# Attention and feed-forward on one core: two weight chunks begun later, and a group's last quarter product done in halves

## The chip, the cores and the metric

The kernel runs on one core of a Trainium2 chip. The metric is the device time of one execution in microseconds (us). The time of a kernel is the median of several executions; besides them there is one execution under the hardware profiler, which gives the profile and the trace.

The core has five engines that run their own instruction queues in order: PE (TensorE, matmuls), DVE (VectorE), ACT (ScalarE), POOL (GpSimd) and SP (SyncE, here only an issuer of DMAs). They meet at semaphores: an instruction that needs another engine's result waits at the head of its queue, and all behind it waits too. Matmul results land in PSUM[...].

## The reference

```python
scores = scale * np.matmul(q, k.transpose(0, 1, 3, 2))          # (8, 8, 576, 576)
thresh = np.max(scores, axis=-1, keepdims=True) - tau
scores = np.where(scores >= thresh, scores, -1000000000.0)
scores = scores - np.max(scores, axis=-1, keepdims=True)
attn = np.exp(scores)
attn = attn / (np.sum(attn, axis=-1, keepdims=True) + 1e-09)
x = np.matmul(attn, v)                # then heads side by side: (8, 576, 512)
xn = (x - mu) / np.sqrt(var + 1e-06) * g_ln
out = x + np.maximum(xn @ w_ch1, 0.0) @ w_ch2                   # 512 -> 2048 -> 512
```

There are 8 batches of 8 heads with 576 tokens of 64 features, in float32. The mean and the variance go over the 512 features of a token. The two weight matrices come in as 64-bit values and have to be turned into float32 on the chip, once.

## The kernel before, in words

**Slots.** A batch has nine slots, so there are 72 slots, n = 0 to 71. Each slot has the scores of a part of the queries for two heads (`scores`, L404; the scores of all slots lie in the same PSUM banks), their maxima and exponentials (`exponentials`, L427, four ACT instructions e0 to e3), thresholds and sums (`weights`, L451: four DVE instructions "STT", L456, which read the scores a second time), and in the next slot the turned weights times v. In the first slots of the kernel the weights are turned on PE: the products named tr and tp go to PSUM and ACT copies them to the tiles em (L500, L506) that the values' product reads. In later slots this goes through a DRAM scratch, scr.

**Groups.** The feed-forward part works on 16 groups g of 288 tokens (two per batch). `first_part` (L781) makes 16 tiles of hidden, each four products p1 and a ReLU on ACT (L801). Group 0 then multiplies with w2 in the plain way (`second_plain`). All other groups use `second_quarters` (L844): w2 and hidden are each seen as 2 x 2 quarters, and seven products of quarters (a scheme of Strassen's kind) take the place of eight. They are the seven calls of `segment`: w2[0,0], w2[0,1], s3, s2, w2[1,1], w2[1,0], and s4 last, where s2, s3, s4 are differences of w2's quarters. Each `segment` is a sum over d = 0..7 for two tiles m = 0, 1 of 144 columns, both in one PSUM bank; a `product` is two instructions of 64 rows and [...] a segment has 64 matmul records in the trace. ACT copies the whole bank out (L896). In the last group, g = 15, the s4 segment is instead multiplied by the root of the variance on DVE (`times_root`). The pool `ps_ff`, from which the segments, p1, the means and the variances take their PSUM banks, holds two.

Additions of the seven results to the quarters of y (u2, u3, u4, 11, 12, 21, 22), the scaling and the residual (`finish`) and the transposes for the output (`store`, into tiles ot, L722) are put off: `later` hangs them on a list, `drops`, with an engine and a cost, and `drip` takes a few from it at fixed places of a slot (with everything=True all of them). `send` (L725) issues four DMAs for each 128 features. They go on SP's queue; for the last group they are spread over SP, ACT and POOL.

**Order.** The order is written out by hand in the main loop (L1062 to L1148): each engine's queue has the instructions in the order in which that code emits them. Each slot has four positions, and at each `second_part` (L993) lets the feed-forward steps of the current group run, as many as a budget says. Where a slot's parts are put off into the next slot, `at_quarter` notes the position, and `run` emits them there. In slots 1 to 4 some products on constants (`constants`, L1054) stand ahead of the scores.

**Weights.** Class `Weights` (L178) converts 32 chunks of 512 columns, 16 of w1 and then 16 of w2. One chunk is a load on SP (`fetch`), two DVE instructions (`begin`, L274 and L278), two ACT instructions (queued by `begin`, L284 and L287, let go by `flush`), an addition on POOL (`carry`, L299), a mask on DVE (`mask`, L308) and, for w1 only, a scaling on POOL (`scale`, L320). Table `BEGUN` (L1049) says for each slot how many chunks are begun by three positions of the slot: ahead of the STTs, behind them (there the next slot's scores run on PE), and at the slot's end. Masks are emitted ahead of the STTs (L1093) and behind them (L1108). A group's products wait for the chunks they need.

Of the kernel before, what the change touches and what calls it, by code (L numbers as in the profile page):

```python
# [12 lines left out]
ALU = mybir.AluOpType  # L13
# [5 lines left out]
def kernel(  # L19
# [76 lines left out]
    def product(out, lhsT, rhs, **flags):  # L96


        for h in range(2):
            r = slice(64 * h, 64 * h + 64)  # L100
            nc.tensor.matmul(out[r], lhsT=lhsT[:, r], rhs=rhs, **flags)  # L101
# [325 lines left out]
    def exponentials(n):  # L427


        neg = small.tile([128, 4], F32, tag="neg", name="neg")  # L430
        thr = small.tile([128, 4], F32, tag="thr", name="thr")
        es = e_room[(n + 1) % 2 if n < SLOTS else 0]
        for h in range(2):
            i = slice(2 * h, 2 * h + 2)
            nc.vector.tensor_reduce(  # L435
                out=neg[:, i], in_=pairs[h],
                axis=AXL.X, op=ALU.max, negate=True,
            )
            nc.gpsimd.tensor_scalar(  # L439
                out=thr[:, i], in0=neg[:, i], scalar1=-1.0, scalar2=low_sb,  # L440
                op0=ALU.mult, op1=ALU.add,
            )
            if h == 0:
                run(n, "copy")
                conversion.scale_all()
        for i in range(4):
            if i == 2:
                yield es, thr
            nc.scalar.activation(es[:, i], blocks[i], func=AF.Exp, bias=neg[:, i : i + 1])  # L449

# [237 lines left out]
    def drip(room=None, everything=False):  # L688


        urgent = [i for i, d in enumerate(drops) if d[0]]
        n = urgent[-1] + 1 if urgent else 0
        room = dict(room or {})
        while drops:
            _, when, eng, cost, go = drops[0]
            if n <= 0 and not everything:
                if when == now or room.get(eng, 0) < cost:
                    break
                room[eng] -= cost
            drops.pop(0)  # L700
            n -= 1
            go()
# [17 lines left out]
    def store(eng, g, m, o):  # L720
        ot = ffn.tile([128, TOK], F32, tag="o", bufs=4, name="ot")
        eng.transpose(ot, o)  # L722
        stores.append(lambda: send(g, m, ot))

    def send(g, m, ot):  # L725
        b, t = divmod(g, 2)
        for i in range(4):
            f = m * 128 + 32 * i
            eng = nc.sync
            if g == NG - 1:  # L730
                eng = (nc.sync, nc.gpsimd)[m % 2] if m >= HM else (nc.sync, nc.scalar)[i % 2]
            eng.dma_start(
                out=out[b, t * TOK : (t + 1) * TOK, f : f + 32].rearrange(
                    "(n r) c -> r n c", r=32
                ),
                in_=ot[32 * i : 32 * i + 32].rearrange("p (n c) -> p n c", c=32),
            )
# [106 lines left out]
    def second_quarters(g, rb):  # L844

        s2, s3, s4 = more
        b11, b12 = hidden[:, :HD, early], hidden[:, :HD, late]  # L850
        b21, b22 = hidden[:, HD:, early], hidden[:, HD:, late]
        drip(everything=True)
        y = ffn.tile([128, NK, TOK], F32, tag="sq", bufs=1, name="y")
        part_of = lambda t, i, j: t[:, HM * i : HM * i + HM, (early, late)[j]]
        y11, y12, y21, y22 = (part_of(y, i, j) for i in range(2) for j in range(2))
        done = set()

        def later(*calls, urgent=None):
            for what, cost, fn, eng, *args in calls:

                def go(what=what, fn=fn, eng=eng, args=args):
                    fn(eng, *args)
                    done.add(what)

                drops.append((urgent, now, eng, cost, go))

        def need(*what):
            while not done.issuperset(what):
                drops.pop(0)[-1]()

        def by_fours(eng, out, in0, in1, op):
            for d in range(0, HD, 4):
                at = (slice(None), slice(d, d + 4))
                eng.tensor_tensor(out=out[at], in0=in0[at], in1=in1[at], op=op)  # L874

        def times_root(out, bank):
            r = rb[:, late].unsqueeze(1).to_broadcast([128, HM, HT])
            dve.tensor_tensor(out=out, in0=bank, in1=r, op=ALU.mult)

        def segment(weights, rhs, out=None, as_it_is=False):  # L880
            bank = ps_ff.tile([128, HM, HT], F32, tag="ff", name="seg")
            for d in range(HD):
                for m in range(HM):
                    at, end = (d, m), (HD - 1, HM - 1)
                    product(
                        bank[:, m], lhsT=weights[:, m, d], rhs=rhs[:, d],
                        start=at == (0, 0), stop=at == end,
                    )
                    if at != end:
                        yield 2, 0.5  # L890
            if out is None:
                out = ffn.tile([128, HM, HT], F32, tag="part", bufs=4, name="part")
            if as_it_is:
                times_root(out, bank)
            else:
                nc.scalar.copy(out, bank)  # L896
            return out

        def add(eng, out, a, b):
            eng.tensor_tensor(out=out, in0=a, in1=b, op=ALU.add)  # L900

        def finish(eng, i, j=None):

            cols = slice(None) if j is None else (early, late)[j]
            at = (slice(None), slice(HM * i, HM * i + HM), cols)
            z, x = y[at], groups[g][at]
            r = rb[:, cols].unsqueeze(1).to_broadcast(list(z.shape))
            eng.tensor_tensor(out=z, in0=z, in1=r, op=ALU.mult)
            add(eng, z, z, x)

        dve, pool = nc.vector, nc.gpsimd
        done_by = pool if g < NG - 1 else dve
        later(("t3", 3, by_fours, pool, b12, b22, b12, ALU.subtract), urgent=pool)
        banks_taken[0] = True
        yield from segment(w2[0, 0], b11, y11)
        need("t3")
        later(("t2", 3, by_fours, dve, b11, b11, b12, ALU.add), urgent=dve)
        yield 2, 0.5
        p2 = yield from segment(w2[0, 1], b21)
        need("t2")  # L920
        later(("t4", 3, by_fours, pool, b21, b21, b11, ALU.subtract), urgent=pool)
        yield 2, 0.5
        p7 = yield from segment(s3, b12)
        yield 2, 0.5
        yield from segment(s2, b11, y21)
        need("t4")
        later(("t1", 3, by_fours, dve, b11, b22, b11, ALU.subtract), urgent=dve)
        later(
            ("u2", 1, add, pool, y21, y21, y11), ("11", 1, add, pool, y11, y11, p2),
            ("done11", 2, finish, pool, 0, 0),  # L930
        )
        yield 2, 0.5
        p4 = yield from segment(w2[1, 1], b21)
        yield 2, 0.5
        need("t1", "u2", "11")
        p5 = yield from segment(w2[1, 0], b11)
        later(
            ("u4", 1, add, dve, y12, y21, p5), ("u3", 1, add, dve, y21, y21, p7),
            ("22", 1, add, dve, y22, y21, p5), ("21", 1, add, dve, y21, y21, p4),
            ("hi", 3, finish, done_by, 1),  # L940
        )
        ends_here = g == NG - 1
        if ends_here:
            later(("done12", 2, finish, dve, 0, 1))
            later(*((f"o{m}", 1, store, dve, g, m, y[:, m]) for m in (2, 3)))
        yield 2, 0.5
        last = segment(s4, b22, as_it_is=ends_here)
        for _ in range(12):
            yield next(last)
        banks_taken[0] = False  # L950
        while waiting_mean:
            mean_of(waiting_mean.pop(0))
        p3 = yield from last
        later(("12", 1, add, dve, y12, y12, p3))
        if not ends_here:
            later(("done12", 2, finish, done_by, 0, 1))
        later(
            *((f"o{m}", 1, store, dve, g, m, y[:, m]) for m in ((2, 3, 0, 1) if g < NG - 1 else (0, 1)))
        )
        yield 2, 0.5  # L960

    def ffn_steps(g):
# [73 lines left out]
    else:  # L1036
# [10 lines left out]
        conversion.scaled = conversion.n1  # L1047

    BEGUN = [  # L1049
        (0, 0, 2), (3, 3, 4), (5, 5, 6), (7, 7, 8), (9, 9, 10), (11, 11, 12),  # L1050
        (14, 16, 18), (20, 22, 24), (26, 28, 30), (32, 32, 32),
    ]

    def constants(times):  # L1054
# [7 lines left out]
    for n in range(NS):  # L1062
# [27 lines left out]
            conversion.fetch(2)  # L1090
        if n < SLOTS + HP:
            run_all(aside)
        conversion.mask_all()  # L1093
        conversion.begin_to(masks_at)
        if n <= HP + 1:
            conversion.carry_all()
# [92 lines left out]
```

## Time and profile before

| | us |
|---|---|
| median of three executions | 1358.27 (1357.86, 1358.27, 1360.97) |
| the profiled execution | 1357.61 |
| its span, first to last instruction | 1355.8 |
| PE busy in the span | 1326.8 (98%) |
| DVE, POOL, ACT busy | 874.0, 615.3, 470.0 |
| first matmul to the end of slot-wise conversion, about | 0 to 189.3 |
| last matmul ends | 1346.33 |

The profiled execution is 1.8 us longer than its span, which runs from the first to the last instruction. The clock that the throttle granted to TensorE was 0.998 of full speed over the span.

How to read the lines of the profile. A row of the waits names an engine, what it wanted to do, and what released it; then the waited time in all, the number of waits and the longest one. A row of the timeline has a start and a length in us, engine, line, operation, output<-inputs with their sizes, the number of instructions of that kind that were put together, and in brackets the idle time just before with its releaser. L101 is the helper `product`, through which all the feed-forward products go, so these are told apart by the tile's name: p is p1 or p2, seg is a segment, mean and var are the layernorm's sums. seg<-hidden,e is the s4 segment, because s4 is kept in the room of a former e tile.

### The profile page before, as it was taken

How to read it: one execution, taken by the hardware profiler on the slowest of the kernel's cores; microseconds unless marked ns; L12 is line 12 of the kernel's file. 1: busy time of each engine (PE TensorE's matmuls, PEld its weight loads, DVE VectorE, ACT ScalarE, POOL GpSimd, SP SyncE). 2: the span in 40 equal slices, each digit the busy share in tenths (PEclk: the TensorE clock that was granted, in tenths of full speed). 3: DMA queues.
4: the chain of work that ended last, by engine and by line, in shares of the span. 5: the costliest groups of instructions: out<-in, count | busy, mean ns of one | idle time of the engine just before them, and what ended most of it. 6: DMA issues, size and time to landing. Idle time of an engine off the chain costs nothing.

```text
span 1355.8 us, 40852 instructions
## 1 busy us (share of the span) xinstructions
PE 1326.8 (98%) x17616; PEld 1003.3 (74%) x17616; DVE 874.0 (64%) x1531; ACT 470.0 (35%) x1022; POOL 615.3 (45%) x824
## 2 busy tenths in 40 slices
PE   8999999999999999999999999999999999999997
PEld 6766657869687786968778696877869687786967
DVE  7978777666755676666766667556766667665202
ACT  4877432332423323232333323233232323333120
POOL 3554455445444344444534454443444445344312
PEclk9999999999999999999999999999999999999999
DMA  9813464457644775447744576446754376443211
GB/s 172 264 52 98 122 182 148 177 159 183 190 141 142 194 197 167 150 136 183 195 149 151 150 191 180 147 146 188 201 169 150 131 189 178 144 155 131 64 19 19
DMA packets 320996, 206.88 MB, mean 153 GB/s; under 512 B 246896, under 2 KB 278384, under 8 KB 312752
## 3 DMA queue, kind: packets, MB, share of 16 engines
q1 hardware_dynamic: 314704, 203.38, 52.0%
q8 instruction: 138, 2.26, 0.7%
q10 hardware_dynamic: 5952, 0.74, 0.4%
q0 software_dynamic: 160, 0.15, 0.1%
q14 instruction: 42, 0.34, 0.1%
HBM read 120.46 MB, written 83.76 MB: 151 GB/s over the span
## 4 chain that ended last, share of the span: by engine, by line
PE 90%; DVE 3%; ACT 2%; DMA 1%; POOL 1%; issue 1%; SPq 1%; POOLq 0%; DVEq 0%; ACTq 0%
PE p L101 37%; PE seg L101 30%; PE sc L421 10%; PE sc L604 8%; PE sc L614 2%; PE tp L101 1%; ACT e L449 1%; DVE e L456 1%; PE var L101 1%; PE mean L101 1%; SPq L118 0%; DMA x_room<-in_moe_w_ch_dram 0%; ACT em L506 0%; DMA qk_room<-in_q_dram 0%; DVE w L308 0%
## 5 line engine op out<-in xcount | busy, mean ns | idle before, releaser
L101 PE MATMUL p<-xc,w 128*64 128x288 f32 x4096 | 517.4, 408 | 6.8 <-ACT part L896 4.6
L101 PEld LDWEIGHTS p<-xc,w 128*64 128x64 f32 x4096 | 287.4, 137 | 214.4 <-issue 13.5
L435 DVE TENSOR_REDUCE neg<-sc 128x2 f32<-128x1152 f32 x144 | 188.6, 1351 | 280.8 <-PE sc L421 280.2
L472 POOL TENSOR_SCALAR e<-e,den 128x576 f32<-128x576 f32 x252 | 193.6, 780 | 133.5 <-DVE den L461 133.5
L101 PE MATMUL seg<-hidden,w 128*64 128x144 f32 x3840 | 247.9, 287 | 0.0
L101 PEld LDWEIGHTS seg<-hidden,w 128*64 128x64 f32 x3840 | 234.9, 137 | 11.5 <-issue 8.5
L456 DVE SCALAR_TENSOR_TENSOR e<-sc,thr,e 128x576 f32<-128x576 f32 x288 | 221.8, 809 | 16.9 <-POOL thr L439 11.2
L801 ACT ACTIVATE hidden<-p 128x288 f32<-128x288 f32 x256 | 106.6, 417 | 303.6 <-PE p L101 303.6
L439 POOL TENSOR_SCALAR thr<-neg,low_sb 128x2 f32<-128x2 f32 x144 | 41.4, 288 | 374.4 <-DVE neg L435 374.0
L449 ACT ACTIVATE e<-sc,neg 128x576 f32<-128x576 f32 x288 | 197.9, 755 | 2.4 <-DVE neg L435 2.4
L546 DVE STREAM_TRANSPOSE et<-e 128x1152 f32<-128x1152 f32 x112 | 153.4, 1374 | 14.7 <-POOL e L472 14.2
L421 PE MATMUL sc<-kT,qT 64*64 64x384 f32 (+3 forms) x2048 | 139.4, 403 | 3.2 <-DVE e L456 2.2
L604 PE MATMUL sc<-em,v_in 128*64 128x128 f32 (+1 forms) x2368 | 129.4, 263 | 0.0
L604 PEld LDWEIGHTS sc<-em,v_in 128*64 128x64 f32 x2368 | 122.8, 137 | 7.9
L101 PE MATMUL seg<-hidden,stage 128*64 128x144 f32 x1920 | 123.3, 286 | 0.0
L101 PEld LDWEIGHTS seg<-hidden,stage 128*64 128x64 f32 x1920 | 117.6, 137 | 2.9 <-issue 2.9
L627 ACT COPY x<-sc 128x128 f32<-128x128 f32 x120 | 31.7, 266 | 238.8 <-PE sc L421 170.4
L421 PEld LDWEIGHTS sc<-kT,qT 64*64 64x64 f32 x2048 | 76.1, 133 | 44.1 <-issue 21.2
L874 POOL TENSOR_TENSOR hidden<-hidden 128x576 f32<-128x576 f32 x60 | 84.8, 1426 | 52.1 <-ACT hidden L801 42.4
L896 ACT COPY part<-seg 128x288 f32<-128x288 f32 x74 | 29.9, 404 | 190.4 <-PE seg L101 190.0
L874 DVE TENSOR_TENSOR hidden<-hidden 128x576 f32<-128x576 f32 x60 | 51.3, 889 | 51.5 <-PE seg L101 48.5
L101 PE MATMUL seg<-hidden,e 128*64 128x144 f32 x960 | 65.3, 286 | 0.0
(145 smaller groups left out, 1098.9 us busy)
## 6 DMA issues: line engine op xcount, KB each, us to landing
scr<-et SPq DMA_DIRECT2D x63, 1152.0 KB, 4.9
em<-scr SPq DMA_DIRECT2D x63, 1024.0 KB, 5.7
q_in<-in_q_dram SPq DMA_DIRECT2D x124, 72.0 KB, 2.7
out_dram<-ot SPq DMA_DIRECT2D x248, 36.0 KB, 3.8
k_in<-in_k_dram SPq DMA_DIRECT2D x120, 72.0 KB, 3.0
er<-scr SPq DMA_DIRECT2D x126, 64.0 KB, 5.2
v_in<-in_v_dram SPq DMA_DIRECT2D x28, 256.0 KB, 5.5
w<-in_moe_w_ch_dram SPq DMA_DIRECT2D x12, 512.0 KB, 4.8
```

What stands on the lines that cost most here:

```text
L101: nc.tensor.matmul(out[r], lhsT=lhsT[:, r], rhs=rhs, **flags)
L421: nc.tensor.matmul(sc[h][64 * i : 64 * i + 64, at : at + n], lhsT=ql[r] if s == HP else qT[r, half, j * 128 + 64 * i : j * 128 + 64 * i + 64],
L435: nc.vector.tensor_reduce(out=neg[:, i], in_=pairs[h], axis=AXL.X, op=ALU.max, negate=True,)
L439: nc.gpsimd.tensor_scalar(out=thr[:, i], in0=neg[:, i], scalar1=-1.0, scalar2=low_sb, op0=ALU.mult, op1=ALU.add,)
L449: nc.scalar.activation(es[:, i], blocks[i], func=AF.Exp, bias=neg[:, i : i + 1])
L456: nc.vector.scalar_tensor_tensor(out=es[:, i], in0=blocks[i], scalar=thr[:, i : i + 1], in1=es[:, i], op0=ALU.is_ge, op1=ALU.mult, accum_o ...
L472: nc.gpsimd.tensor_scalar(out=es[:, i], in0=es[:, i], scalar1=den[:, i : i + 1], scalar2=1.0, op0=ALU.mult, op1=ALU.mult,)
L546: nc.vector.transpose(et[:, :, 64 * h : 64 * h + 64].rearrange("p n (j c) -> p j n c", j=2), es[:, 2 * h : 2 * h + 2].rearrange("p j (n c) ...
L604: nc.tensor.matmul(dst[64 * h : 64 * h + 64], lhsT=vt[:, h, c, :], rhs=pick(em[:, 2 * j : 2 * j + 2, c], h), start=c == 0 and first, stop= ...
L627: nc.scalar.copy(x_of(2 * b + (s > HP))[:, s % (HP + 1), 128 * j : 128 * j + 128], pv[j])
L801: nc.scalar.activation(hidden[:, d], p1, func=AF.Relu)
L874: eng.tensor_tensor(out=out[at], in0=in0[at], in1=in1[at], op=op)
```

## The change

There are three parts.

1. `exponentials` gives control back after its third exponential, not its second, in slots 1 to 5. ACT then has e2 ahead of the copies that are emitted at the slot's first position.
2. `BEGUN` begins one chunk fewer in each of slots 1 and 2, stays two behind through slot 6, and makes up for them with a third chunk in the middle of slots 7 and 8. In slots 0 to 2 no masks are emitted ahead of the STTs; what is due there comes behind the STTs, into the gap in which the next scores run.
3. In `second_quarters` the s4 segment runs over m outside and d inside. After m = 0 is complete, `end_of_half` copies its 144 columns on ACT (line 902 of the changed kernel), and after m = 1 the other 144. In the last group each half is multiplied, added, transposed and handed to `send` at once on DVE (line 905), after all that is put off has been let go. The sums are in another order: 21 and u3 come after the p4 segment, 22 and u4 after p5, and the last group's finishes are split into three. The s2 segment is copied to y12 instead of y21. The last group's sends go to SP alone for m = 2, 3, and to SP, ACT, POOL, SP for m = 0, 1.

```diff
-            if i == 2:
+            if i == (3 if 0 < n < HP + 2 else 2):
                 yield es, thr
...
-            if g == NG - 1:
-                eng = (nc.sync, nc.gpsimd)[m % 2] if m >= HM else (nc.sync, nc.scalar)[i % 2]
+            if g == NG - 1 and m < HM:
+                eng = (nc.sync, nc.scalar, nc.gpsimd, nc.sync)[i]
...
-        def times_root(out, bank):
-            r = rb[:, late].unsqueeze(1).to_broadcast([128, HM, HT])
-            dve.tensor_tensor(out=out, in0=bank, in1=r, op=ALU.mult)
-
-        def segment(weights, rhs, out=None, as_it_is=False):
+        def segment(weights, rhs, out=None, halves=None):
             bank = ps_ff.tile([128, HM, HT], F32, tag="ff", name="seg")
-            for d in range(HD):
-                for m in range(HM):
-                    at, end = (d, m), (HD - 1, HM - 1)
-                    product(
-                        bank[:, m], lhsT=weights[:, m, d], rhs=rhs[:, d],
-                        start=at == (0, 0), stop=at == end,
-                    )
-                    if at != end:
-                        yield 2, 0.5
+            at = [(d, m) for d in range(HD) for m in range(HM)]
+            if halves:
+                at.sort(key=lambda t: t[1])
             if out is None:
                 out = ffn.tile([128, HM, HT], F32, tag="part", bufs=4, name="part")
-            if as_it_is:
-                times_root(out, bank)
+            for i, (d, m) in enumerate(at):
+                product(
+                    bank[:, m], lhsT=weights[:, m, d], rhs=rhs[:, d],
+                    start=d == 0 if halves else i == 0,
+                    stop=d == HD - 1 if halves else i == len(at) - 1,
+                )
+                if i == len(at) - 1:
+                    break
+                if halves and d == HD - 1:
+                    halves(m, out[:, m], bank[:, m])
+                yield 2, 0.5
+            if halves:
+                halves(m, out[:, m], bank[:, m])
             else:
                 nc.scalar.copy(out, bank)
             return out
+
+        def end_of_half(m, out, bank):
+            if not ends_here:
+                nc.scalar.copy(out, bank)
+                return
+            drip(everything=True)
+            dve.tensor_tensor(out=out, in0=bank, in1=rb[:, late], op=ALU.mult)
+            add(dve, y12[:, m], y12[:, m], out)
+            store(dve, g, m, y[:, m])
+            run_all(stores)
...
-        yield from segment(s2, b11, y21)
+        yield from segment(s2, b11, y12)
...
         p4 = yield from segment(w2[1, 1], b21)
+        later(("u3", 1, add, dve, y22, y12, p7), ("21", 1, add, dve, y21, y22, p4))
+        if ends_here:
+            later(("done21", 2, finish, dve, 1, 0))
...
         p5 = yield from segment(w2[1, 0], b11)
-        later(
-            ("u4", 1, add, dve, y12, y21, p5), ("u3", 1, add, dve, y21, y21, p7),
-            ("22", 1, add, dve, y22, y21, p5), ("21", 1, add, dve, y21, y21, p4),
-            ("hi", 3, finish, done_by, 1),
-        )
+        later(("22", 1, add, dve, y22, y22, p5), ("u4", 1, add, dve, y12, y12, p5))
         if ends_here:
-            later(("done12", 2, finish, dve, 0, 1))
-            later(*((f"o{m}", 1, store, dve, g, m, y[:, m]) for m in (2, 3)))
+            later(
+                ("done22", 2, finish, dve, 1, 1), ("done12", 2, finish, dve, 0, 1),
+                *((f"o{m}", 1, store, dve, g, m, y[:, m]) for m in (2, 3)),
+            )
+        else:
+            later(("hi", 3, finish, pool, 1))
         yield 2, 0.5
-        last = segment(s4, b22, as_it_is=ends_here)
+        last = segment(s4, b22, halves=end_of_half)
...
     BEGUN = [
-        (0, 0, 2), (3, 3, 4), (5, 5, 6), (7, 7, 8), (9, 9, 10), (11, 11, 12),
-        (14, 16, 18), (20, 22, 24), (26, 28, 30), (32, 32, 32),
+        (0, 0, 2), (2, 2, 3), (3, 3, 4), (5, 5, 6), (7, 7, 8), (9, 9, 10),
+        (12, 14, 16), (19, 21, 23), (26, 28, 30), (32, 32, 32),
     ]
...
-        conversion.mask_all()
+        if n >= HP - 1:
+            conversion.mask_all()
         conversion.begin_to(masks_at)
```

## Prediction

> **What bounds the kernel now.** I read the busy shares first, then the chain that ended last, then TensorE's waits, then the timeline around each place that the change touches.
>
> ```profile
> PE 1326.8 (98%) x17616; PEld 1003.3 (74%) x17616; DVE 874.0 (64%) x1531; ACT 470.0 (35%) x1022; POOL 615.3 (45%) x824
> ```
> ```profile
> PE 90%; DVE 3%; ACT 2%; DMA 1%; POOL 1%; issue 1%; SPq 1%; POOLq 0%; DVEq 0%; ACTq 0%
> ```
>
> PE is busy for 98% of the span and makes 90% of the chain. So only three things can move the time: the 1355.8 - 1326.8 = 29 us in which PE is idle, new PE idle time, and PE work (the instructions are the same in number and shape, so none). The stretches by window say where the 29 us lie: about 14.7 us before 189.3 us, 5.1 us from there to the last matmul (1157.03 - 1152.06 = 5.0 in the row of 189.30 to 1346.33), 9.5 us after it.
>
> ```profile
> PE p L101 <- ACT part L896: 4.6, 8, 0.6
> PE tr L520 <- ACT em L506: 2.8, 5, 0.7
> PE tp L101 <- ACT em L506: 2.4, 4, 0.8
> PE sc L421 <- DVE e L456: 2.2, 5, 0.6
> PE p L101 <- DVE w L308: 1.4, 1, 1.4
> ```
>
> These are TensorE's waits. In the long steady part there is one kind only, the first, eight times: a group's first product waits until ACT has copied the s4 segment out of PSUM, because the p1 and segment banks come from a pool of two. The other four kinds lie in the first 189 us. One of the eight, closer:
>
> ```profile
> 416.14 3.11 PE L101 MATMUL seg<-hidden,e 128*64 128x144 f32 x48
> 419.57 1.15 PE L101 MATMUL seg<-hidden,e 128*64 128x144 f32 x16
> 420.84 0.40 ACT L896 COPY part<-seg 128x288 f32<-128x288 f32 x1 [2.79 <-PE seg L101]
> ```
>
> The columns are start, length, engine, line and operation. This is the s4 segment: 64 matmuls of 144 columns, one each 3.11/48 = 0.065 us, with a mean product between the 48th and 49th. The next waiting product starts at 421.29. The last pair of matmuls started at 420.43, so without a wait the next would have started at 420.43 + 2 x 0.065 = 420.56: **the price of one full PE -> ACT -> PE round trip with a 128x288 copy is 421.29 - 420.56 = 0.73 us**, of which the copy itself is 0.40.
>
> **What the Trainium skill says.** "PSUM — Partial Sum Buffer", section "PSUM bank collisions raise a hardware error": two engines may not touch one bank and quadrant at once, and PSUM is to be guarded by bank and quadrant, not by address. The trace of before shows no engine reading a bank that PE still fills; the segment copy starts 0.12 us after the last matmul's end. Same page, "Engine vs sequencer instructions": matmuls start and complete in program order; so nothing queued behind a waiting one passes it, and in the trace p waits with all that follows. "Perfetto Trace Analysis", "Optimizing Scalar/DVE Operations": each ACT or DVE instruction has a fixed overhead, and larger ones are better where the engine is full, smaller ones where another waits. The trace agrees: ACT's copies from PSUM took 0.215, 0.266, 0.404 and 0.594 us at 64, 128, 288 and 512 columns. "DMA: Bandwidth & Descriptors", "Issuing engines are not separate DMA queues": issuing from several engines saves only issue time. No run shown here separates the two.
>
> **Part 1: the halves of s4 (groups 1 to 15).** Before, d ran outside and m inside, so both halves of the bank were open to the end. Now m = 0 is finished after 32 of the 64 matmuls, is copied, and m = 1 goes on in the same bank. I built the changed kernel and resolved its waits: in all 15 groups the 33rd matmul waits for that half's reader, ACT in groups 1 to 14 and DVE in the last. Before, the segment had a wait at its start only. The first 48 matmuls stand without anything between them in each of the 15 groups (the x48 row above), so nothing lies at the boundary to cover it. Cost: a round trip with a 128x144 copy. By the rows just named that copy takes about 0.28 us (between 0.266 at 128 and 0.404 at 288), so 0.73 - (0.404 - 0.28) = **0.61 us**. ACT must also be free. Half time of 416.14 is 418.2; the p5 copy of ACT started at 417.61 and took 0.44, so it is free at 418.05. In group 1 ACT is in two exponentials until 260.36 while the half ends at about 259.8 plus latency: 0.93 us. So 13 x 0.61 + 0.93 = +8.8 us. Both ends: if a wait cost only the 0.12 between matmul end and copy start, 14 x 0.12 = +1.7; if ACT is caught in an exponential (0.755 mean) in half the groups, 0.35 more for 7 of them, +11.3. I take +8.8, because the same round trip was measured eight times at 0.57 of wait, each time alike. It is partly given back: the second half's copy at the segment's end is short too, so the eight waits shown lose 0.12 each: -1.0. What moves because of the reordered sums (u3 and 21 after p4, 22 and u4 after p5) is queued on DVE at 64% with half a segment of room, and nothing on PE waits for it before the group's end: 0.
>
> **Part 2: slots 1 to 9, in order.** I followed PE's position against before. The exponential moved ahead of ACT's em copies costs 0.635 us of ACT (its pitch) wherever a transpose waits on that copy, and makes the third weight STT earlier, for which the scores wait. The masks of slots 1 and 2 go from ahead of the STTs to behind them, where DVE has nothing else until the next scores are done. A PE-bound slot of the loop (scores to turns 4.33, turns to scores 4.57, scores 2.19: 11.09, against 11.06 measured) hardly gains. Running sum: slot 2's scores -0.65 (the masks leave the way), slot 3's 0, slot 4's +0.6 (transposes wait for em behind the exponential), slot 5's 0, slot 6's -0.6, which shrinks to -0.2 where a mean waits for POOL's sum. Slot 7 gets a third conversion, one more pair of ACT instructions of 0.576 us each = 1.15, and PE was waiting on ACT here already:
>
> ```profile
> 116.47 0.46 PE L101 MATMUL p<-xc,w 128*64 128x288 f32 x2 [0.73 <-ACT hidden L801]
> ...
> 160.36 0.33 PE L520 MATMUL tr<-diag,e 128*64 128x128 f32 x2 [0.69 <-ACT em L506]
> ...
> 179.22 0.46 PE L101 MATMUL p<-hidden,w 128*64 128x288 f32 x2 [1.37 <-DVE w L308]
> ```
>
> These three are the rows of the timeline where PE waits on the conversion or beside it. After the first: +0.9. A wait of 0.77 at 153.34 goes with the earlier reduction: +0.2. In slot 9 all three last conversions (3 x 1.15 = 3.46 of ACT, where one of 1.15 stood) come between o's copy and em4's; PE there had 0.70 of slack: the second row comes at about 162, +1.7. Then the third row's 1.37 goes, since the last mask is earlier and the last load no longer stands behind an scr store on SP: **+0.3 net**. This is my least certain sum: down to -4.3 if all of DVE's waits (2.2 + 0.77 + 1.37) go and the exponential costs nothing; up to +3 if slots 7 to 9 pay for each pair.
>
> **Part 3: the end.**
>
> ```profile
> 1342.24 4.09 PE L101 MATMUL seg<-hidden,e 128*64 128x144 f32 x64
> ...
> 1347.76 5.46 SPq L732 DMA_DIRECT2D out_dram<-ot  x8
> 1348.01 0.42 DVE L878 TENSOR_TENSOR part<-seg,rb 128x288 f32<-128x288 f32 x1
> ...
> 1349.01 0.84 DVE L722 STREAM_TRANSPOSE ot<-y 128x288 f32<-128x288 f32 x2
> ```
>
> Before: PE ends at 1346.33, DVE at 1349.85, the last send is issued at about 1352.8, the span ends 3.0 later. After: DVE's queue holds, from 1342.96, the two adds, two finishes and two transposes for m = 2, 3 and only then half 0's multiply. By the durations of before that is 2 adds at 1.93/4 = 0.97, two finishes of a multiply (0.45) and an add (0.46) = 1.82, the transposes 0.83 and the half multiply some 0.3: 3.9, so it ends at about 1346.9. PE's 33rd matmul waits for it: the second half runs 1347.0 to 1349.05 (PE ends 2.7 later). Half 1's multiply, add and transpose at half size take about 1.1, so the last tile is ready at 1350.15, 0.3 later than before. But SP issues 12 sends from 1346.33 at about 0.47 each, the last near 1351.6 against 1352.8, and ACT and POOL two each: **-1.1** (from -2 to +0.5, where the late tile sets the end instead).
>
> **The sum.** 8.8 - 1.0 + 0.3 - 1.1 = +7.0 on the profiled execution's 1357.61 (span 1355.8, 1.8 around it): 1364.6. The median of the runs, 1358.27, is 0.66 above that execution; a change of 7.0 on it gives **1365.3 us**, slower by 0.5%. A measurement here tells about 0.3%, 4.1 us, from no change.
>
> **Rivals.**
> (a) Not slower: the start was bound by DVE, so the 4.3 us go and the earlier exponential is free. For: the five sc<-DVE waits are in consecutive slots, which a single queue would make. Against: tr and tp wait on ACT as often. 8.8 - 1.0 - 1.1 - 4.3 = +2.4: 1360.7. That is not slower as measured. It decides from a start gain of 2.9 us on. Chance 0.14.
> (b) The start loses 3 more, as the ACT pairs of slots 7 to 9 stand ahead of PE's copies and the last w1 chunk's scale comes late: 1368.3. For: ACT's three queued pairs. Against: the 1.37 wait must go. Chance 0.2.
> (c) The half waits cost next to nothing (PE's queue hides the copy): 0.12 x 14 - 1.0 - 1.1 with 4 of the start's 4.3 gained = -4.4, so 1353.9, the faster side. For: the split lets sums begin earlier. Against: the same round trip is seen at 0.57 eight times, with full queues. Chance 0.05.
> (d) In the last group DVE's queue holds PE longer than the sends save: +1 instead of -1.1: 1367.4. Chance 0.1; the rest, 0.51, is the forecast.
>
> **How the numbers follow.** The slower side by over 4.1 us holds the forecast, (b) and (d), 0.81; within 0.3% is (a), 0.14; faster is (c), 0.05. Range: from (a), 1361, to (b) with part of the ACT end, 1369; outside it about 0.2.
>
> **What would show it.** Right: in the changed profile, 14 new rows of PE waiting on ACT's half copy in the seg product, mean near 0.45 to 0.6, and one wait of about 2.5 on DVE near 1346; steady-part PE idle up by about 8 us; the eight p waits shorter by 0.12; no w wait at 179; the last SP send near 1351.6 plus the shift. Wrong: seg waits absent or under 0.2, or first-189-us idle changed by more than 3 us either way.

## The result, and the profile after

The changed kernel takes 1370.83 us (median of four, 1370.27 to 1372.82) against 1358.32 before: a ratio of 1.0091 with a 95% interval of 1.0073 to 1.0108, or +12.5 us. The forecast was +7.0 (1365.3) with a range up to 1369. So the direction was right and the size was not. The profiled execution is the slowest of the four, 1372.82 with a span of 1371.0.

The page of the changed kernel, its busy line and its chain:

```profile
PE 1334.7 (97%) x17616; PEld 1005.7 (73%) x17616; DVE 877.0 (64%) x1535; ACT 472.8 (34%) x1036; POOL 618.8 (45%) x822
```
```profile
PE 86%; ACT 1%; DVE 1%; issue 1%; POOL 0%; POOLq 0%; ACTq 0%; DVEq 0%
```

PE still carries the chain and has the same 17616 matmuls, but its busy time has risen by 7.9 us. A count that stays while its time rises is worth a second look; it comes up again below. TensorE's waits after:

```profile
PE seg L101 <- ACT part L902: 6.6, 14, 0.7
PE tr L520 <- ACT em L506: 6.4, 5, 2.1
PE p L101 <- ACT part L902: 3.0, 8, 0.4
PE p L101 <- ACT hidden L801: 3.0, 1, 3.0
...
PE seg L101 <- DVE part L905: 2.1, 1, 2.1
PE p L101 <- POOL w L299: 1.9, 1, 1.9
```

The first row is the wait that the forecast named, 14 times at 0.47 (6.6/14). The third row is the old p wait, 3.0/8 = 0.38 where it was 0.57. The last group's wait on DVE is there, 2.1. The wait on the last mask in slot 10 (1.4 before) has gone. Rows that no step of the forecast had are a single wait of 3.0 on a ReLU and one of 1.9 on POOL.

**Where the 15.2 us of span lie.** The s4 segments are anchors that both traces have. That of group 1 starts at 257.72 before and 265.20 after: **+7.48 in the start**. From there to the s4 of the last group it is 1084.52 before and 1092.69 after: **+8.17 in the body**. From there to the end of the span it is 13.56 and 13.11: **-0.45 at the end**. The forecast had +0.3, +7.8 (8.8 - 1.0) and -1.1.

One segment of the body, in group 3, from the timeline of the changed kernel:

```profile
425.06 2.13 PE L101 MATMUL seg<-hidden,e 128*64 128x144 f32 x32
...
426.53 0.44 ACT L897 COPY part<-seg 128x288 f32<-128x288 f32 x1
...
427.32 0.28 ACT L902 COPY part<-seg 128x144 f32<-128x144 f32 x1 [0.35 <-PE seg L101]
...
427.65 1.20 PE L101 MATMUL seg<-hidden,e 128*64 128x144 f32 x16 [0.46 <-ACT part L902]
```

Before, 48 matmuls stood in one row. Now PE stops after 32, ACT copies 0.28 us (the forecast's estimate was 0.28), and PE goes on 0.46 after the end of its 32nd. Both halves lie in one bank, the piece of PSUM that a tile of the pool `ps_ff` takes.

The body's 8.17 us are 6.6 of these waits, less 4.6 - 3.0 = 1.6 for the shorter p waits, and 3.1 of PE's busy time: 1079.57 us of the body before, 1082.71 after, with the clock at full speed in both. So a pause costs some 0.2 us more than its wait row shows (3.1/14, an estimate).

**The start, slot by slot.** The scores' start in slot n, after minus before, is -0.07 in slot 3, +0.55 in slot 4 (+1.18 in slots 5 and 6, where a wait in the middle of the scores goes, so that their end is at +0.55), +4.80 in slot 7, +7.01 in slots 8 and 9, +9.07 in slot 10, +7.48 in slot 11. So slots 6, 7 and 9 lose 4.3, 2.2 and 2.1, and slot 10 gives 1.6 back. In these slots the changed kernel's timeline has:

```profile
93.51 1.66 POOL L320 TENSOR_SCALAR w<-hidden,g_sb 128x512 f32<-128x512 f32 x1
...
95.20 0.41 ACT L801 ACTIVATE hidden<-p 128x288 f32<-128x288 f32 x1 [2.46 <-POOL w L320]
...
95.67 4.33 PE L101 MATMUL p<-xc,w 128*64 128x288 f32 x20 [2.96 <-ACT hidden L801]
...
122.48 1.19 PE L101 MATMUL p<-xc,w 128*64 128x288 f32 x8 [1.86 <-POOL w L299]
...
167.80 1.12 PE L520 MATMUL tr<-diag,e 128*64 128x128 f32 x8 [2.11 <-ACT em L506]
```

Read upward from the PE row of slot 6. PE waits for a ReLU of group 0, the ReLU waits for POOL, and POOL's operands say why: it scales a w1 chunk out of the room of the tile hidden, which the ReLU is about to write. In the kernel that room may hold chunks 0 to 9 while they are converted. Before, slot 6 was at chunks 10 and up when group 0 began; two chunks behind, it is still at chunk 9. In slot 7 PE waits for POOL's carry and scaling of the last w1 chunks, which before had been scaled well ahead. In slot 9 it waits behind the three pairs of ACT conversions.

The windows of the 4 us after each of these three waits add the piece that explains PE's busy time (columns: window, length, then busy time and count for PE, PEld, DVE, ACT, POOL, then the granted clock):

```profile
95.67:99.67 4.00, 4.00 (x20) 2.12 (x22) 3.11 (x4) 1.58 (x4) 1.35 (x1) 0.57 0.00 0
122.48:126.48 4.00, 3.45 (x30) 1.90 (x32) 3.83 (x7) 2.10 (x5) 2.39 (x2) 1.00 0.12 13
167.80:171.80 4.00, 4.00 (x24) 2.52 (x26) 3.79 (x11) 0.37 (x1) 4.00 (x5) 0.58 0.02 4
```

After the waits of 2.96 and 2.11 the granted clock is near half, and PE is "busy" with half the work. It stands at 0.50 from 96.06 to 99.47 and from 167.74 to 171.16, 3.41 us, and costs 1.71 us both times. With the second half of the last s4, which takes 3.83 us at half clock for the 2.13 of the first, these stretches make 2 x 1.71 + 1.70 = 5.1 of the 7.9 us more of PE's busy time; the body's 3.1 are the rest, within 0.3. Slot 6's 4.3 are then 2.96 - 0.40 (the same place waited 0.40 before) + 1.71.

### The profile page after: what moved, and what is told of

Its sections match the earlier page's. It is cut to its first block, busy times and chain, and to the rows that moved or that the text cites. A ratio compares the mean times of both kernels' runs of the same rounds, so it can differ in the third digit from the quotient of the medians.

```text
span 1371.0 us, 40883 instructions
## 1 busy us (share of the span) xinstructions
PE 1334.7 (97%) x17616; PEld 1005.7 (73%) x17616; DVE 877.0 (64%) x1535; ACT 472.8 (34%) x1036; POOL 618.8 (45%) x822
## 4 chain that ended last, share of the span: by engine, by line
PE 86%; ACT 1%; DVE 1%; issue 1%; POOL 0%; POOLq 0%; ACTq 0%; DVEq 0%
PE p L101 36%; PE seg L101 30%; PE sc L421 9%; PE sc L604 8%; PE sc L614 2%; PE var L101 1%; PE mean L101 1%; ACT part L902 0%; ACT e L449 0%; DVE y L911 0%; DVE neg L435 0%; DVE w L308 0%; ACT et L284 0%; PE tr L520 0%; ACT stage L287 0%
## 5 line engine op out<-in xcount | busy, mean ns | idle before, releaser
L456 DVE SCALAR_TENSOR_TENSOR e<-sc,thr,e 128x576 f32<-128x576 f32 x288 | 222.2, 810 | 17.9 <-POOL thr L439 11.7
L101 PE MATMUL seg<-hidden,e 128*64 128x144 f32 x960 | 69.9, 292 | 8.7 <-ACT part L902 6.6
L101 PEld LDWEIGHTS seg<-hidden,e 128*64 128x64 f32 x960 | 60.7, 139 | 15.5 <-ACT part L902 10.4
```

What stands on the lines that cost most here:

```text
L456: nc.vector.scalar_tensor_tensor(out=es[:, i], in0=blocks[i], scalar=thr[:, i : i + 1], in1=es[:, i], op0=ALU.is_ge, op1=ALU.mult, accum_o ...
```

## The experiments

All times are against the kernel before, run on the same chip each time (1358.0 to 1358.2).

**Two halves of the question.** The first theory was that the shared bank makes the body's loss and the late weight chunks make the start's. Part 3 alone and parts 1 and 2 alone were run, and two repairs of the whole.

*Part 3 alone* (`exponentials`, `BEGUN` and the masks as before).

> The kernel before with part 3 alone (halves of s4, sums in the new order, sends); the start is as before. Theory A (the trace of the changed kernel: 8.2 us of its rise lie between the s4 segments of groups 1 and 15, and the end gains 0.45): 1358.3 + 0.8 for group 1's own wait + 8.2 - 0.45 = 1366.8, and 14 rows of seg waiting on ACT's half copy at 0.47 each. Rival B (the waits are mostly covered, and the start makes nearly the whole rise): at most 1361.

Measured 1364.83, ratio 1.0051 (1.0038 to 1.0065): +6.8. Its body is 1092.64 long, 8.12 more than before, and its end 12.24, 1.32 less; the start is +0.1. Rival B falls. The expectation was 2 too high, mostly because it counted group 1's wait twice (it lies inside the 8.2) and took the end from the one profile of the changed kernel. The forecast of these parts, +7.8 and -1.1, is within 0.4 of both.

*Parts 1 and 2 alone.*

> The kernel before with parts 1 and 2 alone (third exponential first, chunks begun later, masks behind the STTs). Theory A (the start loses 7.5 us in the profiled execution, which was itself 2 us above the others): 1358.3 + 5 to 7.5 = 1363 to 1366, with the same waits in slots 6, 7 and 9. The blind forecast for this part was +0.3: 1358.6. Rival B would have it at 1368 or more.

Measured 1364.85, ratio 1.0050 (1.0038 to 1.0063): +6.8, where +0.3 was forecast. Its trace has the waits of 2.95, 1.86 and 2.13 in slots 6, 7 and 9. So parts 1 and 2 cost as much as part 3, and the two together (13.6) somewhat more than the change (12.5).

*The changed kernel without chunks 8 and 9 in hidden's room.*

```diff
-                (hidden, 4, lambda p: 10),
+                (hidden, 4, lambda p: 8),
```

> The changed kernel, but chunks 8 and 9 may not be made in the room of the tile hidden (they take another piece). Theory A (ACT's fourth ReLU of group 0 in slot 6 waits until POOL has scaled chunk 9 out of hidden's room, and the PE clock drops after that wait): the wait of 2.96 us goes back to about 0.4 and the slow stretch after it goes: 1370.8 - 2.6 - 1.7 = 1366.5. Rival C (ACT's exponential placed first makes the start late, whatever the rooms): 1370.8.

Measured 1370.32, ratio 1.0094 (1.0080 to 1.0108): no gain that can be told. The mechanism was right and its worth was not. The wait of 2.96 is 0.39 now and slot 7 starts 4.26 earlier than in the changed kernel, as expected. But then PE waits more on POOL's scaling in slot 7, the transposes wait 2.15 in slot 9 as before, and in slot 10 the wait on the last mask is back:

```profile
PE p L101 <- DVE w L308: 1.5, 1, 1.5
...
PE p L101 <- POOL w L320: 1.1, 2, 0.9
```

In its profile 1.9 us are left of the gain at group 1's s4. One late chunk repaired leaves the chain of chunks as late as it was.

*The changed kernel with a bank of its own for the second half.*

```diff
                 if halves and d == HD - 1:
                     halves(m, out[:, m], bank[:, m])
+                    bank = ps_ff.tile([128, HM, HT], F32, tag="ff", name="seg")
```

> The changed kernel, but the second half of s4 has a PSUM bank of its own, in all 15 groups. Theory A (the waits in s4 come from the one bank): the 14 waits of 0.47 go, and the last group's of 2.06 with the slow stretch after it, of which the end gives back what its sends allow, about 1: 1370.8 - 6.6 - 1 = 1363.2. Rival D (it is the order of the products, m outside and d inside, that costs): 1370.8.

Measured 1361.61, ratio 1.0027 (1.0017 to 1.0037), 9.2 below the changed kernel (9.0 when each is set against its own runs of the kernel before). The order of the products is as in the changed kernel and all the waits in s4 are gone, so rival D falls and the one bank is the cause. The body is 1083.38: 9.31 us for 14 waits, 0.66 each, where 0.61 (and once 0.93) was forecast. The expectation had counted the 6.6 us of the waits' rows and not their whole price, and so was 1.6 too high. In this profile the wait of 2.94 in slot 6 is not followed by the slow clock, and group 1's s4 starts 1.5 earlier.

**Which part of the start, and the clock.**

*Part 1 alone, the third exponential first.*

> The kernel before with part 1 alone, the third exponential ahead of ACT's em copies in slots 1 to 5. Theory A' (the late weight chunks make the start's loss, and a slot 10 wait of 1.37 on the last mask absorbs part of what earlier slots lose): +0.2 to +1.2, 1358.9. Rival C (the exponential makes the loss): 1363 to 1365.

Measured 1359.30, ratio 1.0006 (0.9998 to 1.0015): +1.1, which the interval doesn't tell from nothing. Its trace shows a cost all the same: tr waits 1.23 us in four slots in a row (0.60 before), the cycle of these slots is 11.7 instead of 11.07, and 1.9 us are lost by group 1's s4. The forecast's running sum had two such losses of 0.6 and then gave both back by slot 6; here they stay.

*Part 2 alone, chunks later and masks behind the STTs.*

> The kernel before with part 2 alone, chunks begun later and masks behind the STTs. Theory A': slot 2 gains 0.7, then the waits on POOL in slot 6 and 7 and on ACT in slot 9 with their slow stretches: +5.5 to +7, 1364. Rival C: at or below 1359.

Measured 1361.45, ratio 1.0027 (1.0017 to 1.0037): +3.3. Slot 6's scores come 1.3 earlier than before, so part 2 does bring what it was read to bring there, and then slots 6, 7 and 9 take it back with the waits of 2.95, 1.89 and 2.13. The two parts alone sum to 4.4 and together make 6.8. In the profiles 1.7 of that difference is one slow stretch of the clock, which part 2 alone doesn't have after its wait in slot 6:

```profile
93.79:97.79 4.00, 4.00 (x48) 3.01 (x50) 3.13 (x4) 2.99 (x6) 2.01 (x2) 1.00 0.00 0
118.94:122.94 4.00, 3.47 (x32) 1.93 (x34) 3.83 (x7) 2.12 (x5) 2.37 (x2) 1.00 0.08 22
164.26:168.26 4.00, 4.00 (x24) 2.54 (x26) 3.79 (x11) 0.37 (x1) 4.00 (x5) 0.57 0.02 4
```

The same wait of 2.95 is followed by 48 matmuls in 4 us at full clock here, and by 20, most of them at half clock, in the changed kernel.

*When does the clock fall?* This kernel is part 3 alone with idle ACT copies ahead of the first half's copy, a number per group.

```diff
+                for _ in range(STALLS[g] if m == 0 else 0):
+                    nc.scalar.copy(idle, ident)
                 nc.scalar.copy(out, bank)
```

> The halves-only kernel, with 2 to 9 copies of a 128x128 constant put on ACT ahead of the first half's copy in groups 1 to 14 (the result is unchanged), so that PE's 14 waits in s4 last about 0.47 + 0.32 for each copy, 1.1 to 3.4 us. It asks when PE's clock falls after a wait. Theory E (the clock is judged in windows that don't begin with the wait): waits under about 1.9 are never followed by half clock, waits near 2.1 to 2.7 only in some places, waits over 3.3 in all. Rival F (the wait's length alone decides): a sharp length, near 2.0, above which every wait is followed by half clock at the same delay.

Measured 1375.17, a single execution. The copies partly ran while ACT was waiting anyway, so only some waits became long: 2.84, 2.18, 1.93, 1.54, 1.19 and shorter. Windows after the two longest:

```profile
584.23:588.73 4.50, 4.12 (x48) 3.12 (x50) 2.77 (x6) 0.28 (x1) 0.49 (x1) 1.00 0.00 0
745.79:750.29 4.50, 4.32 (x36) 3.37 (x36) 2.06 (x5) 0.14 (x1) 1.15 (x2) 0.62 0.01 4
```

The wait of 2.84 is not followed by half clock and that of 2.18 is, from 0.8 us after PE's restart on. Rival F falls: the length alone does not decide. Theory E is borne out for the short waits (no drop after any of up to 1.93 in all traces here) and for the middle ones; no wait over 3 us came about, so its last claim wasn't tried.

What decides can be worked out from the traces. Within each of the 13 traces all changes of the granted clock lie whole multiples of 3.41 us apart (in the changed kernel, for instance, at 96.06, 99.47, 167.74, 171.16, 1362.41 and 1365.82). Cut into windows on that grid, the same wait looks different in two kernels. The changed kernel, then part 2 alone:

```profile
92.65:96.06 3.41, 0.45 (x6) 0.30 (x6) 3.38 (x4) 0.95 (x3) 2.52 (x2) 1.00 0.00 0
96.06:99.47 3.41, 3.41 (x18) 1.75 (x16) 2.72 (x4) 0.99 (x4) 1.35 (x1) 0.50 0.00 0
```
```profile
89.32:92.73 3.41, 1.52 (x14) 0.62 (x10) 2.26 (x2) 1.57 (x5) 3.41 (x3) 1.00 0.00 0
92.73:96.14 3.41, 2.35 (x20) 1.46 (x22) 3.34 (x5) 2.00 (x5) 1.92 (x2) 1.00 0.00 0
```

In the first the wait of 2.96 falls into one window, which leaves PE 0.45 us of work, and the next window is at half clock. In the second the wait of 2.95 is cut into 1.89 and 1.06, and the clock stays. Likewise the wait of 2.18 above lies in one window and that of 2.84 is cut into 1.38 and 1.46. From the first record of the clock to the last matmul, 12 windows at full clock in the 13 traces had PE idle for 2.05 us or more, and each was followed by half clock; all others had it idle for 1.89 or less, and none was.

*Part 2's relief, caught up in slot 5.*

```diff
-                (hidden, 4, lambda p: 10),
+                (hidden, 4, lambda p: 8),
...
-        (0, 0, 2), (3, 3, 4), (5, 5, 6), (7, 7, 8), (9, 9, 10), (11, 11, 12),
+        (0, 0, 2), (2, 2, 3), (3, 3, 4), (5, 5, 6), (7, 7, 8), (9, 11, 12),
...
-        conversion.mask_all()
+        if n >= HP - 1:
+            conversion.mask_all()
```

> The kernel before with part 2's relief of slots 1 and 2 (one chunk fewer, masks behind the STTs), but caught up in slot 5 instead of slots 7 and 8, and chunks 8 and 9 kept out of the tile hidden's room. Theory A' (part 2 costs because the chunks are late in slots 6 to 9, not because of what it moves in slots 1 and 2): the waits of 2.95 (ReLU), 1.89 (POOL) and 2.13 (transposes) go, the wait on the last mask in slot 10 is back and takes what the early slots gain: 1357.5 to 1358.5. Rival G (moving the masks or the rooms costs by itself): 1361 as with part 2 alone.

Measured 1357.91, ratio 0.9998 (0.9990 to 1.0006): no difference. All three waits are gone, the wait on the last mask in slot 10 is 1.38 again, and the 1.3 us won by slot 6 are lost to a mean that waits 1.46 and to later slots. Rival G falls; with the chunks on time again, part 2 costs nothing, and brings nothing.

**A faster version, and two misses.**

*Part 3 alone with two banks.*

> The kernel before with part 3 alone and a bank of its own for the second half of s4. Theory A (only the shared bank cost): eight waits of p shorter by 0.12 to 0.2, no wait in s4, the end shorter by 1.3: 1358.1 - 1.1 - 1.3 = 1355.7, faster than before. Rival D (the reordered sums or sends cost too): 1358 or more.

Measured 1355.13 (13 runs), ratio 0.9975 (0.9967 to 0.9983): faster than before by 3.0 us. Its segment in group 3, from its timeline:

```profile
416.35 3.16 PE L101 MATMUL seg<-hidden,e 128*64 128x144 f32 x48
...
417.82 0.44 ACT L898 COPY part<-seg 128x288 f32<-128x288 f32 x1
...
418.60 0.28 ACT L903 COPY part<-seg 128x144 f32<-128x144 f32 x1 [0.35 <-PE seg L101]
...
419.34 0.66 PE L101 MATMUL mean<-sum,avg_sb 128*64 128x288 f32 x4
```

The copy of half 0 at 418.60 lies beside PE's 48 matmuls, and the bank that the second half takes is the one whose copy ends at 417.82 + 0.44 = 418.26, just in time. The body is 1.07 shorter than before and the end 1.55 (13.56 to 12.01).

*The same with the masks of slots 0 to 2 behind the STTs.*

> The two-bank kernel with the old start, which took 1355.1, and of part 2 only the masks of slots 0 to 2 behind the STTs, with all chunks begun as before. If the early slots' gain reaches the end: 1354.4. If the wait on the last mask in slot 10 takes it: 1355.1.

Measured 1355.66 (1354.56 to 1358.58), ratio 0.9984 (0.9978 to 0.9991): nothing gained. Its profile has no wait on the last mask, but a wait of 2.11 on em in slot 9 with the slow clock after it, so neither of the two expected ways came. Why the mask's place alone brings that wait was not followed further.

*The changed kernel with the last group's multiply first.*

```diff
-            drip(everything=True)
             dve.tensor_tensor(out=out, in0=bank, in1=rb[:, late], op=ALU.mult)
+            drip(everything=True)
```

> The changed kernel, but in the last group the first half's multiply stands ahead of what was put off on DVE, not behind it. Theory A (PE waits 2.06 us for that multiply, and the clock drops behind it in some executions; the sends on SP take a part of the gain): wait under 0.7, no slow stretch, 1370.8 - 1 = 1369.8. Rival H (SP's twelve sends alone set the end): 1370.8.

Measured 1371.83, ratio 1.0103 (1.0088 to 1.0119): no gain. PE's wait fell from 2.06 to 0.48 and the slow stretch there is gone, but the end became 14.0 us long, longer than the 13.11 of the changed kernel. The rows that say why, and last the sends of the changed kernel for comparison:

```profile
1358.45 0.31 DVE L904 TENSOR_TENSOR part<-seg,rb 128x144 f32<-128x144 f32 x1 [4.08 <-PE seg L101]
...
1361.63 5.86 SPq L732 DMA_DIRECT2D out_dram<-ot  x12
...
1363.29 0.48 DVE L722 STREAM_TRANSPOSE ot<-y 128x288 f32<-128x288 f32 x1
```
```profile
1361.50 6.46 SPq L732 DMA_DIRECT2D out_dram<-ot  x12
```

DVE stood still for 4.08 us at the multiply, with the adds and finishes behind it that could have run meanwhile. So SP's first send starts 5.43 us after the last s4 does (1356.20), in place of 3.61 in the changed kernel (1357.89). From there the twelve sends take 5.86 us, and they end 3.7 us after DVE's last transpose (1367.49 against 1363.77). Rival H had the right queue, SP's, but not that its start would move; Theory A's saving on PE doesn't reach the end.

## Why the prediction was off, point by point

- **Part 1 of the working, the halves of s4: right.** 14 waits of 0.47 on ACT and one on DVE, where the built program had them. Price 0.66 in place of 0.61 each, the p waits shorter by 0.19 in place of 0.12; body +8.17 against +7.8. These two misses have opposite signs, so a part of the sum's closeness is luck. PE's idle time in the body rose by 5.0 us and not by the 8 that the forecast gave as a sign; the other 3.1 are counted as busy. The two-bank kernel shows the cause by taking it away. The Trainium skill ("PSUM — Partial Sum Buffer", section "PSUM bank collisions raise a hardware error") says to guard PSUM by bank and quadrant and not by address. The traces agree: PE waited 0.47 for the copy of other columns of the bank that it was to fill, and with a second bank it did not wait.
- **Part 2 of the working, slots 1 to 9: this is the step that failed.** It ended at "+0.3 net" and its upper bound was +3; it measured +7.48 in the profile and +6.8 in the run with parts 1 and 2 of the change alone. PE's idle time in the first 189.3 us rose from 14.6 to 19.1 (up to the same work, 7.48 later), over the 3 us that the forecast gave as a sign of being wrong. Four terms of its running sum were off:
  - The exponential: the running sum was -0.65, 0, +0.6, 0 and -0.6 in slots 2 to 6. By the end of the scores it was -0.71, -0.09, +0.55, +0.55 and +0.55. The two losses of 0.6 were read rightly; the two gains of 0.6 after them did not come (part 1 of the change alone lost 1.9 by group 1).
  - Slot 6: "shrinks to -0.2". A ReLU waits 2.46 us on POOL there for the room of hidden, +2.56 on PE. The forecast followed engines' queues and PE's inputs, not who else had the ReLU's output tile. The changed program has this dependence in it, so it could have been found beforehand.
  - Slot 7: "+0.9" for a pair of ACT instructions. It was the last w1 chunks' carry and scaling on POOL, 1.86 and 0.39 and 0.16 in place of 0.73, +2.2 with what follows.
  - The clock: two stretches at half clock, 1.71 each. The forecast had no term for it.
  - Right were slot 2's gain (0.7), the wait of 0.77 that goes, the 1.4 added in slot 9 (1.5 forecast), and the 1.37 that goes in slot 10.
- **Part 3 of the working, the end: right in sign.** -0.45 in the changed kernel's profile and -1.32 with part 3 of the change alone, -1.1 forecast. PE's wait on DVE was 2.06.
- **The rivals.** (b) named the place and the mechanism (ACT pairs in slots 7 to 9, the last w1 chunks' scaling late) with 3 more; it was 7 more. It had a chance of 0.2. (a) and (c) fell, (d) too: the end was no longer than before. (In (a) the start gain from which it decides is 6.7 - 4.1 = 2.6 us and not 2.9.)

So the mechanism that carried most of the forecast held, and the range failed because the least certain sum was bounded by counting known waits, while the delay of two chunks ran into other users of those chunks and of their rooms.

## What to carry to other kernels

When a step is done later, list what its buffers do next as well as who needs its result: a tile lent as a workspace can make its owner wait. Before an accumulation is split so that one part can be read early, look which bank each part lies in; here part 3 of the change cost 6.8 us with both halves in one PSUM bank and won 3.0 with two. And an estimate made of several small shifts along one queue of work has a range much wider than the sum of its terms, since a wait that goes can uncover or make another.

## What the runs showed of the hardware

A wait of PE of 2.06 to 2.96 us was followed by half clock in some executions and not in others: yes after 2.11, 2.12, 2.13, 2.15, 2.18 and 2.96, no after 2.07, 2.84 and 2.94, both ways after 2.06 and 2.95, and never after 1.93 or less. Where it could be seen whole, the stretch lasted 3.41 us and lost 1.71, and it began between 0.1 before and 1.2 us after the restart. The wait of 2.06 in the last group shows the range: in the changed kernel the clock fell 0.3 us after the restart and the second half of s4 took 3.83 us, with part 3 of the change alone it fell 1.2 after and the half took 2.97, and in the kernel with the idle copies it didn't fall and the half took 2.18.

The Trainium skill ("TensorE: Matmul & The Clock Gate", "Part 1: The HAM clock gate (the "warmup" mystery)") says that the activity window is about 3.4 us long and free-running. The traces agree: the clock changes on a grid of 3.41 us, and its records begin between 5.3 and 7.6 us after the first instruction, so that the grid lies differently in each execution. The page puts the drop after at least one idle window; here a window with PE idle for 2.05 of its 3.41 us was enough, and one with 1.89 was not. So a wait costs its length, and 1.71 us more where at least 2.05 us of it fall into one window, which for the waits of 2.06 to 2.96 here was a matter of phase.
